# A cached-attention decode layer on one Trainium2 core: the query weights' rows are dealt to the partitions in another way

## The chip, the cores and the metric

One core of a Trainium2 chip runs the kernel. The metric is the device time of one execution in microseconds: the median of 3 runs was 189.68 us before the change (189.66 to 189.79).

## The reference

One token passes through a layer: normalisation, attention over a cache of 16,384 keys and values in 8 key heads with 32 query heads, and then a block of small matrix products. All inputs are bfloat16.

```python
x = A_x                                             # 1 x 1 x 512
q = _layernorm(x) @ wq                              # wq 512 x 4096; 32 heads of 128
scores = einsum("bhqd,bhkd->bhqk", q, k) * 128 ** -0.5   # k, v: 8 heads x 16384 x 128, each for 4 query heads
o = einsum("bhqk,bhkd->bhqd", softmax(scores), v)
h = x + o.reshape(1, 1, 4096) @ wo                  # wo 4096 x 512
n = _layernorm(h)
x1 = n                                              # plus, with one token, a shifted product that is zero
h2 = _gelu(_layernorm(x1) @ w3) @ w4                # w3 512 x 1792, w4 1792 x 512
out = h + x1 + h2
```

The block B shifts its token by one and two places along a sequence of length one. Nothing but padding is left of it, so the kernel does not read `B_w1` and `B_w2`.

## The kernel before

The kernel is written as one straight list of operations for each engine. A small recorder (`Program`) notes what each operation reads and writes, and puts a semaphore wait ahead of an operation that needs it; TensorE's own list (PE below) is run as a loop. No scheduler moves anything: the order on each engine is the order of the code.

All 17 large loads are issued by SyncE (SP), in this order: the query weights in two pieces, keys of pair 0, values of pair 0, keys of pair 1, values of pair 1 and so on, to pair 3 (whose keys come in two halves), then `wo`, `w3` and `w4`. A "pair" is two key heads; its keys, and its values, are 128 partitions x 64 KB, 8 MB in one load. The input `x` (`x4`, 1 KB as 4 rows of 256 B) is loaded by ScalarE's queue (ACT). A load waits on SP until its destination is free. The buffer `vb` holds first the query weights (`wq_sb` is another name for it) and then the values of each pair, so the values of pair 0 wait for the query product to have read the weights. The keys go into a ring `kb_all`, so the keys of pair 1 wait until VectorE (DVE) has transposed the keys of pair 0.

The start, which the change touches, goes like this. PE copies `x` to all partitions: partitions 32q to 32q+31 hold elements 128q to 128q+127, four quarters in all. `row_sums(0, ...)` takes the sums for the mean and the variance, and transposes `hx` into `hT` in 32 x 32 blocks (L550), so that partition 32q+i holds its four elements 128q + 4i + k, k = 0 to 3. L615 normalises them into `xn`, four columns of 128 elements. L615 also waits for both pieces of the weights: it names `("v", 0)` and `("v", 1)` as read. Then PE makes the query in 32 matmuls (L624): for each of 8 banks, the four columns of `xn` against the four weight rows that lie in the same partition. Partition 32q+i must therefore hold the weight rows that belong to its elements. `variance(0)` and small masks are made on DVE and GpSimd (POOL) in between.

The keys of a pair are transposed on DVE (L647) in pieces of 1024 or 2048 words, multiplied with the query on PE (L666), followed by softmax (L676 to L692), the product with the values (L703) and a gathering of the heads. At the end come the products with `wo` (L795), `w3` (L815) and `w4` (L838, L852). Matmuls at L527 and L535 are never read; they only keep PE busy.

The loads of the weights before:

```python
wq_in = A_wq.rearrange("(p k) c -> p (k c)", k=NCH)
for n, (lo, hi) in enumerate(((0, 2048), (2048, NCH * HQ * DH))):
    load("wq", wq_sb[:, lo:hi], wq_in[:, lo:hi], ("v", 1 - n))
load_keys(0)
```

Partition p holds rows 4p to 4p+3, 32 KB that lie together in memory. The first load takes the first 4 KB of each partition (half of its first row), the second the other 28 KB.

Of the kernel before, what the change touches and what calls it, by code (L numbers as in the profile page):

```python
# [365 lines left out]
HQ = 32  # L366
HKV = 8
SK = 16384
DH = 128
REP = HQ // HKV  # L370
FM = 1792
NCH = D // 128
# [18 lines left out]
def bass_sequential_preLN__gqa_block_cached__mixer_s_mlp__decode_kernel(  # L391
# [13 lines left out]
    with ExitStack() as ctx:  # L405
# [50 lines left out]
        hT = sb("hT", [128, NCH, 32], FP32)  # L456
# [18 lines left out]
        wq_sb, wo_sb = vb, kb[0]  # L475
# [11 lines left out]
        def load(name, dst, src, key, by="SP", also=()):  # L487
            P.op(by, lambda e: e.dma_start(dst, src), w=[key, *also], dma=name)  # L488
# [4 lines left out]
        def load_keys(j, y=None):  # L493
            n = 128 * DH
            if y is None:
                load("k", kb_all[:, BASE[j]:BASE[j] + 2 * n], pair_rows(A_k_cache, j), ("r", 0, 0),
                     also=[("r", y, i) for y in range(2) for i in range(RPARTS) if y or i] + [("tail", j)])
            else:
                load(f"k{y}", kb[y][:, :], pair_rows(A_k_cache, j)[:, y * n:(y + 1) * n], ("r", y, 0),
                     also=[("r", y, i) for i in range(1, RPARTS)])  # L500
# [6 lines left out]
        def dve(fn, r=(), w=(), bank=()):  # L507
            return P.op("DVE", fn, r, w, bank)
# [7 lines left out]
        def pe(fn, r=(), w=(), bank=(), also=()):  # L516

            return P.op("PE", fn, r, w, bank, also=also)

        def piece(cuts, m):  # L520
            return [lo <= m < hi for lo, hi in cuts].index(True)
# [16 lines left out]
        def row_sums(i, row, key):  # L538

            h, hk = (hr, "hr") if i else (hx, "hx")  # L540
            if i:
                dve(lambda e: e.scalar_tensor_tensor(h[:, :], row[:, 0:128], 1.0, hx[:, :], ALU.mult, ALU.add,
                                                     accum_out=rs[i][:, 0:1]),
                    r=[key, "hx"], w=[hk, ("rs", i, 0)], bank=[key])
            else:
                dve(lambda e: e.tensor_scalar(h[:, :], row[:, 0:128], 0.0, 0.0, ALU.add, ALU.add,
                                              accum_out=rs[i][:, 0:1]), r=[key], w=[hk, ("rs", i, 0)], bank=[key])
            dve(lambda e: e.scalar_tensor_tensor(xs[:, :], h[:, :], 1.0, h[:, :], ALU.mult, ALU.mult,
                                                 accum_out=rs[i][:, 1:2]), r=[hk], w=["xs", ("rs", i, 1)])
            dve(lambda e: e.transpose(hT[:, :, :].rearrange("p k u -> p (k u)"),  # L550
                                      h[:, :].rearrange("p (i k) -> p k i", k=NCH)), r=[hk], w=["hT"])
            pe(lambda e: e.matmul(n_ps[:, 0:2], mean4[:, :], rs[i][:, :], start=True, stop=True),
               r=[("rs", i, 0), ("rs", i, 1), "mean4"], w=["n"], bank=["mn"])
            dve(lambda e: e.tensor_copy(st[i][:, 0:2], n_ps[:, 0:2]), r=["n"], w=[(("st", i), 0)], bank=["mn"])
# [15 lines left out]


        load("x4", x4[:, :], A_x[0, 0:1, :].rearrange("o (q j) -> (o q) j", q=4), "x4", "ACT")
        wq_in = A_wq.rearrange("(p k) c -> p (k c)", k=NCH)
        for n, (lo, hi) in enumerate(((0, 2048), (2048, NCH * HQ * DH))):
            load("wq", wq_sb[:, lo:hi], wq_in[:, lo:hi], ("v", 1 - n))
        load_keys(0)

        dve(lambda e: e.memset(mean4[:, :], -1.0 / (32 * D)), w=["mean4"])
# [9 lines left out]
            r=["ident", "x4"], w=["quarter"])  # L588
        pe(lambda e: e.matmul(O_ps[0][:, 0:128], quarter[:, :, :].rearrange("p q u -> p (q u)"), x4[:, :],
                              start=True, stop=True), r=["quarter"], w=[("O", 0)], bank=[("O", 0)])  # L590
        row_sums(0, O_ps[0], ("O", 0))
        variance(0)
        act(lambda e: e.activation(scr[0:1, 0:1], mean4[0:1, 0:1], ACTF.Exp), r=["mean4"], w=["scr"])
# [5 lines left out]
             r=["ident_f"], w=["swapped"])  # L599

        dve(lambda e: e.tensor_reduce(row32[:, :], ident_f[:, :].rearrange("p (c r) -> p r c", c=4), AX.X, ALU.add),
            r=["ident_f"], w=["row32"])
        dve(lambda e: e.tensor_reduce(maskdd[:, :], ident_f[:, :].rearrange("p (n d) -> p d n", d=4), AX.X, ALU.add),
            r=["ident_f"], w=["maskdd"])
# [6 lines left out]
        for z, m, key, mk in ((zo, rowgh, "zo", "rowgh"), (zd, maskgh, "zd", "maskgh")):  # L611
# [5 lines left out]
            r=["hT", (("st", 0), 0), (("st", 0), 6)] + [("v", 0), ("v", 1)], w=["xn"])  # L617
# [3 lines left out]
        for i, key in enumerate(keys):  # L621
            P.part("query", i)
            for k in range(NCH):
                pe(lambda e, k=k: e.matmul(row[:, bass.ds(P.b, 512)], copies(xn[:, k:k + 1], 128),  # L624
                                           wq_k[:, k, bass.ds(P.c, REP * DH)], start=(k == 0), stop=(k == NCH - 1)),
                   r=["xn"], also=[("v", 0), ("v", 1)], w=["n" if key == "mn" else key], bank=[key])
        P.part()
        for g in range(2):
            half = banks[64 * g:64 * g + 64, PAIRS * g:PAIRS * g + PAIRS, :].rearrange("p j c -> p (j c)")
            for b in range(2):  # L630
# [3 lines left out]
                    r=["n" if x == "mn" else x for x in keys[PAIRS * g:PAIRS * g + PAIRS]], w=["qcol"],  # L634
                    bank=keys[PAIRS * g:PAIRS * g + PAIRS])
        for a in range(4):
            lo, hi = 32 * a, 32 * a + 32
# [146 lines left out]
        for n, (lo, hi) in enumerate(W4):  # L784
# [4 lines left out]
            r=[("o_m", j) for j in range(PAIRS)], w=["o_f"])  # L789
# [3 lines left out]
        for r_ in range(32):  # L793
            q = r_ % 4
            pe(lambda e, r_=r_, q=q: e.matmul(O_ps[0][32 * q:32 * q + 32, :], copies(o_b[:, r_:r_ + 1], 32),  # L795
                                              wo_sb[:, r_ * D:(r_ + 1) * D], start=(r_ < 4), stop=(r_ >= 28)),
               r=["o_b", ("r", 0, piece(WO, r_))], w=[("O", 0)], bank=[("O", 0)])
        h_ps, hkey = banks[:, 6, :], "spare0"
        dve(lambda e: e.tensor_copy(osum[:, :], O_ps[0][:, :]), r=[("O", 0)], w=["osum"] + [("osum", c) for c in range(4)], bank=[("O", 0)])
        for q in range(4):  # L800
            pe(lambda e, q=q: e.matmul(h_ps[32 * q:32 * q + 32, 0:128], copies(row32[:, 0:1], 32),
                                       osum[:, q * 128:(q + 1) * 128], start=True, stop=True),
               r=["osum", "row32"], w=[hkey], bank=[hkey])
        s = st[1]
        S = ("st", 1)
        unread(2)
        row_sums(1, h_ps, hkey)
        unread_f(512)
        act(lambda e: e.activation(hc[:, :, :], hT[:, :, :], ACTF.Identity, bias=s[:, 0:1], scale=1.0),
            r=["hT", (S, 0)], w=["hc"])  # L810


        for k in range(NCH):
            for q in range(4):
                pe(lambda e, k=k, q=q: e.matmul(s_ps[32 * q:32 * q + 32, 0, 0:FQ], hc[:, k, :],  # L815
                                                w3_sb[:, k, q * FQ:(q + 1) * FQ], start=(k == 0), stop=(k == NCH - 1)),
                   r=["hc", ("r", 1, piece(W3, k))], w=[("s", 0)], bank=[("s", 0)])
# [3 lines left out]
            r=["hr", "xs", (S, 6)], w=["xsum"])  # L821
        unread_f(384)
        for n in range(2):
            lo, hi = n * NHC // 2, (n + 1) * NHC // 2
# [10 lines left out]
           r=["swapped", "xsum"], w=["n"], bank=["mn"])  # L835
        for m in range(NEAR):
            q = m % 4
            pe(lambda e, m=m, q=q: e.matmul(O_ps[1][32 * q:32 * q + 32, :], hcol[:, m, :], w4_sb[:, m, :],  # L838
                                            start=(m < 4), stop=(m >= NEAR - 4)),
               r=[("hcol", 2 * m // NHC), ("r", 1, len(W3) + piece(W4, m))], w=[("O", 1)], bank=[("O", 1)])  # L840
        dve(lambda e: e.tensor_copy(osum[:, :], O_ps[1][:, :]), r=[("O", 1)], w=["osum"], bank=[("O", 1)])
        act(lambda e: e.activation(hg[:, 0:256], hcol[:, 0:8, :].rearrange("p m u -> p (m u)"), ACTF.Identity),
            r=[("hcol", 1)], w=["late", ("hg", 0), ("hg", 1)])
# [6 lines left out]
        for m in range(NEAR, NHC):  # L850
            for o in range(4):
# [4 lines left out]
                   r=["late", ("r", 1, len(W3) + piece(W4, m))], w=["n"], bank=["mn"])  # L856
        act(lambda e: e.activation(fin[:, 0:128], n_ps[0:64, 0:128], ACTF.Identity),
            r=["n"], w=[("fin", 0)], bank=["mn"])
        dve(lambda e: e.tensor_copy(fin[:, 128:256], n_ps[64:128, 0:128]), r=["n"], w=[("fin", 1)])
        P.op("SP", lambda e: e.dma_start(out[0, 0:1, :].rearrange("o (q j) -> (o q) j", q=2), fin[31:33, :]),  # L860
             r=[("fin", 1), ("fin", 0)], w=["out"], dma="out")
# [32 lines left out]
```

## Time and profile before

| | |
|---|---|
| time, median of 3 | 189.68 us (189.66 to 189.79) |
| time of the profiled execution | 189.68 us |
| its span, first to last instruction | 188.2 us |
| granted TensorE clock, mean | 0.90 |
| PE, DVE, ACT, POOL busy | 127.9, 107.9, 14.2, 9.4 us |
| bytes loaded | 79.17 MB, 421 GB/s over the span |
| SP's DMA queue, share of 16 engines' span | 97.9% |

The page divides the span into 40 slices with the busy share of each engine and of the 16 DMA engines. Behind an issue of a DMA it gives the time to landing, and the chain of waits follows the work back from the last instruction. Each large load consists of one piece per partition and of one small completion packet from each DMA engine that took part; the page counts both as packets.

### The profile page before, as it was taken

The numbers are of one execution on the slowest core, as the hardware profiler recorded it, in microseconds if no ns is written. First come the engines' busy times: TensorE is split into PE (matmuls) and PEld (weight loads), VectorE is DVE, ScalarE is ACT, GpSimd is POOL, SyncE is SP. The second block draws the span as 40 slices with busy tenths as digits, with TensorE's granted clock in tenths as the row PEclk, the third lists the DMA queues.
The fourth block names the chain that finished last, engine by engine and source line by source line (L and its number), as shares of the span: only waits on it lengthen the run. The fifth ranks groups of instructions, "written<-read, shape, count | busy, mean of one in ns | idle before, by whom it ended". The sixth has DMA issues, their size and how long they took to land.

```text
span 188.2 us, 2422 instructions
## 1 busy us (share of the span) xinstructions
PE 127.9 (68%) x776; PEld 53.2 (28%) x780; DVE 107.9 (57%) x138; ACT 14.2 (8%) x32; POOL 9.4 (5%) x21
## 2 busy tenths in 40 slices
PE   1019800699965703999775019997986999797984
PEld 1003300243422201344332003442432334343332
DVE  4300651999645009998450069994659894453254
ACT  3000000000020200000012000000220000320012
POOL 1700000000000020000002100000003000000010
PEclk9999995599997885599999855999998899999999
DMA  6999999999999999888999999997999998799994
GB/s 240 457 418 446 446 446 446 446 446 446 446 446 446 446 446 446 362 376 376 446 446 446 446 446 446 446 446 334 446 446 446 557 446 348 334 471 421 404 410 179
DMA packets 2461, 79.19 MB, mean 421 GB/s; under 512 B 282, under 2 KB 284, under 8 KB 924
## 3 DMA queue, kind: packets, MB, share of 16 engines
q1 hardware_dynamic: 2452, 79.17, 97.9%
q8 instruction: 1, 0.02, 0.0%
q10 hardware_dynamic: 8, 0.00, 0.0%
HBM read 79.17 MB, written 0.00 MB: 421 GB/s over the span
## 4 chain that ended last, share of the span: by engine, by line
DMA 44%; PE 31%; DVE 14%; issue 8%; POOL 1%; SPq 0%; ACT 0%; POOLq 0%; DVEq 0%; ACTq 0%
DMA kb<-in_A_k_cache_dram 30%; PE banks L666 18%; DMA vb<-in_A_v_cache_dram 15%; DVE kt L647 8%; PE banks L527 4%; PE banks L703 4%; DVE pt L692 1%; DVE mx L676 1%; PE banks L795 1%; PE banks L660 1%; DVE od L733 1%; PE banks L680 1%; PE banks L535 1%; PE banks L815 1%; SPq L488 0%
## 5 line engine op out<-in xcount | busy, mean ns | idle before, releaser
L647 DVE STREAM_TRANSPOSE kt<-kb 128x1024 int32<-128x1024 int32 (+1 forms) x49 | 71.8, 1534 | 31.9 <-DMA kb<-in_A_k_cache_dram 31.9
L666 PE MATMUL banks<-kt,qn 128*128 x256 | 67.9, 417 | 0.0
L666 PEld LDWEIGHTS banks<-kt,qn 128*128 x256 | 26.4, 103 | 40.0 <-issue 21.1
L527 PE MATMUL banks<-xn 128*128 128x512 bf16 x90 | 22.0, 381 | 0.6 <-issue 0.6
L660 PE MATMUL banks<-qn 128*128 128x512 bf16 x8 | 3.7, 464 | 26.5 <-DVE kt L647 26.2
L703 PE MATMUL banks<-vb,pt 128*32 128x512 bf16 x256 | 16.3, 411 | 0.0
L624 PE MATMUL banks<-vb,xn 128*128 x32 | 9.2, 459 | 9.6 <-DVE xn L615 9.6
L688 ACT ACTIVATE p_sb<-banks,bias 128x1024 bf16<-128x1024 f32 x4 | 4.5, 1114 | 126.0 <-DVE nmh L684 126.0
L692 DVE STREAM_TRANSPOSE pt<-p_sb 64x1024 bf16<-64x1024 bf16 x8 | 9.9, 1239 | 5.4 <-ACT p_sb L688 5.3
L527 PEld LDWEIGHTS banks<-xn 128*128 128x128 bf16 x94 | 8.8, 99 | 12.1 <-issue 4.5
L676 DVE TENSOR_REDUCE mx<-banks 128x1 f32<-128x1024 f32 x4 | 4.9, 1225 | 9.0 <-PE banks L666 9.0
L703 PEld LDWEIGHTS banks<-vb,pt 128*32 128x32 bf16 x256 | 8.0, 103 | 6.3 <-issue 2.0
L631 DVE STREAM_TRANSPOSE kt<-banks 64x1024 f32<-64x1024 f32 x4 | 4.8, 1227 | 7.2 <-PE banks L624 7.2
L660 PEld LDWEIGHTS banks<-qn 128*128 128x128 bf16 x8 | 0.8, 100 | 28.3 <-issue 28.0
L722 POOL TENSOR_TENSOR osum<-osum 128x256 f32<-128x256 f32 x3 | 2.2, 723 | 127.5 <-ACT osum L719 127.5
L624 PEld LDWEIGHTS banks<-vb,xn 128*128 128x128 bf16 x32 | 3.7, 115 | 14.7 <-issue 12.3
L738 PE MATMUL banks<-od,zo 128*32 128x128 f32 x8 | 1.6, 285 | 7.3 <-POOL od L724 6.1
L680 PE MATMUL banks<-mxd,mean 128*128 128x128 f32 x8 | 2.0, 326 | 5.3 <-DVE mxd L677 5.3
L719 ACT ACTIVATE osum<-banks,rowc 128x128 f32<-128x128 f32 x12 | 3.4, 368 | 20.7 <-PE banks L703 20.7
L615 DVE TENSOR_SCALAR xn<-hT,st 128x4 bf16<-128x4 f32 x1 | 0.3, 290 | 6.5 <-DMA vb<-in_A_wq_dram 6.5
L711 PE MATMUL banks<-acc,zd 128*32 128x1 f32 x8 | 0.9, 180 | 4.1 <-DVE pt L692 4.0
L568 POOL TENSOR_TENSOR st<-st,expo 128x1 f32<-128x1 f32 (+1 forms) x2 | 1.3, 636 | 41.3 <-DVE st L566 41.3
(88 smaller groups left out, 46.3 us busy)
## 6 DMA issues: line engine op xcount, KB each, us to landing
kb<-in_A_k_cache_dram SPq DMA_DIRECT2D x2, 4096.0 KB, 20.4
vb<-in_A_wq_dram SPq DMA_DIRECT2D x1, 3584.0 KB, 11.7
kb<-in_A_wo_dram SPq DMA_DIRECT2D x1, 3584.0 KB, 28.5
kb<-in_B_w_dram SPq DMA_DIRECT2D x1, 1792.0 KB, 24.2
kb<-in_B_w_dram SPq DMA_DIRECT2D x1, 896.0 KB, 26.0
kb<-in_B_w_dram SPq DMA_DIRECT2D x1, 640.0 KB, 27.1
vb<-in_A_wq_dram SPq DMA_DIRECT2D x1, 512.0 KB, 3.6
kb<-in_A_wo_dram SPq DMA_DIRECT2D x1, 512.0 KB, 29.4
```

The source lines that it names most:

```text
L527: P.unread = lambda e: e.matmul(banks[:, 7, :], copies(xn[:, 0:1], 128), copies(xn[:, 0:1], 512), start=True, stop=True)
L624: pe(lambda e, k=k: e.matmul(row[:, bass.ds(P.b, 512)], copies(xn[:, k:k + 1], 128), wq_k[:, k, bass.ds(P.c, REP * DH)], start=(k == 0), s ...
L631: dve(lambda e, g=g, b=b, half=half: e.transpose(qcol[64 * g:64 * g + 64, 2 * b:2 * b + 2, :, :].rearrange("p e m u -> p (e m u)"), half.r ...
L647: P.op("DVE", lambda e, t=t, n=n, at=at: e.transpose(kt[:, t * KP:(t + n) * KP].bitcast(I32), kb_all[:, at:at + n * KP].bitcast(I32)), r=[ ...
L660: pe(lambda e: e.matmul(row[:, bass.ds(P.y, 512)], copies(none, 128), copies(none, 512), start=True, stop=False, skip_group_check=True), r ...
L666: pe(lambda e, n=n: e.matmul(row[:, bass.ds(P.y, 512)], qn[:, n, bass.ds(P.q, 128)], key_piece(P.k, n), start=False, stop=(n == 3), skip_g ...
L676: dve(lambda e: e.tensor_reduce(mx[:, :], s_all, AX.X, ALU.max), r=[("s", 0), ("s", 1)], w=["mx"], **both)
L680: pe(lambda e: e.matmul(m_ps[:, 0:128], mean4[:, :], mxd[:, :], start=True, stop=True), r=["mxd", "mean4"], w=["m"], bank=["mn"])
L688: act(lambda e: e.activation(p_sb[:, :], s_all, ACTF.Exp, bias=bias[:, 0:1], scale=float(SCALE), accum_out=acc[:, :]), r=[("s", 0), ("s", ...
L692: dve(lambda e, g=g: e.transpose(pt[64 * g:64 * g + 64, :, :, g, :], p_sb[64 * g:64 * g + 64, :]), r=["p"], w=["pt"])
L703: pe(lambda e, l=l, ct=ct, ch=ch: e.matmul(O_ps[0][32 * ct:32 * ct + 32, :], pt[:, l, ch, :, :].rearrange("p g u -> p (g u)"), tiles[:, l ...
L719: act(lambda e, c=c: e.activation(osum[:, c * 128:(c + 1) * 128], O[:, c * 128:(c + 1) * 128], ACTF.Identity, scale=rowc[:, c:c + 1]), r=[ ...
```

## The change

The weight rows are dealt out otherwise. Partition 32q+i now holds row 128q+i as its first row, and rows 128q+32+3i to 128q+34+3i as the other three. The first load takes the first row of every partition, whole (8 KB), and the second load the other three (24 KB, which lie together in memory). On the memory side, a load is now described by three dimensions: 4 quarters, 1 MB apart; 32 partitions of each, 8 KB apart in the first load and 24 KB in the second; and the bytes of one partition. Before, it was two: 128 partitions, 32 KB apart, and the bytes. On the side of the partitions there are 128 of them, as before.

The elements of `x` have to follow, so the transposition of `hx` for the first normalisation is cut in two: block 0 (elements 128q+i), and blocks 1 to 3 (elements 128q+32+3i+k). The second call of `row_sums`, at the end of the kernel, stays as it was.

```diff
-            dve(lambda e: e.transpose(hT[:, :, :].rearrange("p k u -> p (k u)"),
-                                      h[:, :].rearrange("p (i k) -> p k i", k=NCH)), r=[hk], w=["hT"])
+            for lo, hi in ((0, NCH),) if i else ((0, 1), (1, NCH)):
+                dve(lambda e, lo=lo, hi=hi: e.transpose(
+                    hT[:, lo:hi, :].rearrange("p k u -> p (k u)"),
+                    h[:, 32 * lo:32 * hi].rearrange("p (i k) -> p k i", k=hi - lo)), r=[hk], w=["hT"])
...
-        wq_in = A_wq.rearrange("(p k) c -> p (k c)", k=NCH)
-        for n, (lo, hi) in enumerate(((0, 2048), (2048, NCH * HQ * DH))):
-            load("wq", wq_sb[:, lo:hi], wq_in[:, lo:hi], ("v", 1 - n))
+        wq_in = A_wq.rearrange("(q d) c -> q d c", q=4)
+        for n, (lo, hi) in enumerate(((0, 1), (1, NCH))):
+            load("wq", wq_sb[:, lo * HQ * DH:hi * HQ * DH],
+                 wq_in[:, 32 * lo:32 * hi, :].rearrange("q (i k) c -> q i (k c)", k=hi - lo), ("v", 1 - n))
         load_keys(0)
```

On SP, at the start of the program, the first loads stand like this (- before, + after; `vb` is the buffer of the weights and values, `kb` that of the keys; the numbers are the destination's shape in elements of 2 bytes):

```order
-L488 DMA vb<-in_A_wq_dram 128x2048
-L488 DMA vb<-in_A_wq_dram 128x14336
+L488 DMA vb<-in_A_wq_dram 128x1x4096
+L488 DMA vb<-in_A_wq_dram 128x1x12288
 L488 DMA kb<-in_A_k_cache_dram 128x32768
 L488 DMA vb<-in_A_v_cache_dram 128x32768
```

Nothing moves in SP's list: still two weight loads, then the keys and the values. Their sizes change from 4 KB and 28 KB of each partition to 8 KB and 24 KB.

On DVE, near the start, `row_sums(0, ...)` and what follows it stood like this before:

```order
L546 TENSOR_SCALAR hx,rs<-banks 128x128
L548 SCALAR_TENSOR_TENSOR xs,rs<-hx 128x128
L550 STREAM_TRANSPOSE hT<-hx 128x128
L554 COPY st<-banks 128x2
L560 SCALAR_TENSOR_TENSOR st<-st 128x1
```

And like this after:

```order
L546 TENSOR_SCALAR hx,rs<-banks 128x128
L548 SCALAR_TENSOR_TENSOR xs,rs<-hx 128x128
L551 STREAM_TRANSPOSE hT<-hx 128x32
L551 STREAM_TRANSPOSE hT<-hx 128x96
L556 COPY st<-banks 128x2
L562 SCALAR_TENSOR_TENSOR st<-st 128x1
```

One transposition has become two, of a quarter and three quarters of the columns. All other rows of every engine stand as before, with line numbers 2 or 3 higher.

## The prediction

> **What bounds the kernel now.** I read the page's DMA part first, because 79 MB in 189.68 us is a lot for one core. The columns are packets, MB, and share of 16 engines' span.
>
> ```profile
> span 188.2 us, 2422 instructions
> DMA packets 2461, 79.19 MB, mean 421 GB/s; under 512 B 282, under 2 KB 284, under 8 KB 924
> q1 hardware_dynamic: 2452, 79.17, 97.9%
> q10 hardware_dynamic: 8, 0.00, 0.0%
> ```
>
> SP's queue (q1) keeps all 16 DMA engines busy for 97.9% of the span. Stretches cut out by the view of windows show whether that is one rate or a mixture (the last two numbers are the share of the DMA engines and GB/s):
>
> ```profile
> 12.95:32.30 19.35, 9.19 (x32) 3.67 (x32) 6.06 (x10) 0.00 (x0) 0.00 (x0) 0.89 1.00 434
> 32.30:70.90 38.60, 26.16 (x146) 10.39 (x147) 22.70 (x21) 2.71 (x7) 1.57 (x3) 0.85 1.00 435
> 101.20:129.00 27.80, 17.64 (x67) 6.91 (x67) 17.90 (x12) 1.50 (x5) 1.57 (x3) 0.82 1.01 434
> 129.00:148.00 19.00, 15.20 (x110) 6.29 (x110) 13.75 (x14) 2.71 (x7) 1.57 (x3) 0.91 1.09 469
> 176.00:186.00 10.00, 7.91 (x101) 3.31 (x102) 4.63 (x16) 1.67 (x4) 0.71 (x1) 1.00 0.96 401
> ```
>
> In the long stretches it is one rate: 434 GB/s at a share of 1.00, 27.1 GB/s for each engine. (The 469 beside a share of 1.09 and the 401 have the edges of large packets in them.) PE and DVE have room in each stretch, so this kernel is a queue of bytes. It stays one only if each load is issued before the one ahead of it has drained. SP's timeline has the issues (start, us, what), and the chain of waits has what they became:
>
> ```profile
> 0.74 0.87 SPq L488 DMA_DIRECT2D vb<-in_A_wq_dram  x2
> 1.66 0.42 SPq L488 DMA_DIRECT2D kb<-in_A_k_cache_dram  x1
> 22.93 0.33 SPq L488 DMA_DIRECT2D vb<-in_A_v_cache_dram  x1
> 45.77 0.33 SPq L488 DMA_DIRECT2D kb<-in_A_k_cache_dram  x1
> 64.26 0.33 SPq L488 DMA_DIRECT2D vb<-in_A_v_cache_dram  x1
> 84.47 0.33 SPq L488 DMA_DIRECT2D kb<-in_A_k_cache_dram  x1
> 101.26 0.33 SPq L488 DMA_DIRECT2D vb<-in_A_v_cache_dram  x1
> 118.67 9.29 SPq L488 DMA_DIRECT2D kb<-in_A_k_cache_dram  x2
> 139.97 0.33 SPq L488 DMA_DIRECT2D vb<-in_A_v_cache_dram  x1
> 147.74 0.80 SPq L488 DMA_DIRECT2D kb<-in_A_wo_dram  x2
> 157.64 1.78 SPq L488 DMA_DIRECT2D kb<-in_B_w_dram  x4
> ```
> ```profile
> 1.66 30.55 DMA kb<-in_A_k_cache_dram
> 45.77 25.13 DMA kb<-in_A_k_cache_dram
> 101.26 27.72 DMA vb<-in_A_v_cache_dram
> ```
>
> An 8 MB load takes 19.35 us at the full rate (the first window holds exactly the keys of pair 0). The second keys took 25.13 us from issue, the third values 27.72, so they stood 5.8 and 8.4 us in the queue. The values of pair 0 were issued at 22.93, 9.3 us before the first keys had landed (1.66 + 30.55 = 32.21). The chain ends in the last weights:
>
> ```profile
> 186.29 0.12 PEld L852 LDWEIGHTS banks<-kb,kt 128*32 128x32 bf16 x8 [0.19 <-DMA kb<-in_B_w_dram]
> ```
>
> PE waits 0.19 us for the last piece of `w4`, 2 us before the end. What lengthens any one engine's queue lengthens the kernel, since a load has landed only when all its engines have.
>
> **How the change alters the loads.** The weights are 512 + 3584 KB in both kernels. The rows of the DMA issues give KB and time to landing:
>
> ```profile
> vb<-in_A_wq_dram SPq DMA_DIRECT2D x1, 3584.0 KB, 11.7
> vb<-in_A_wq_dram SPq DMA_DIRECT2D x1, 512.0 KB, 3.6
> x<-in_A_x_dram ACTq DMA_DIRECT2D x1, 1.0 KB
> out_dram<-kt SPq DMA_DIRECT2D x1, 1.0 KB
> ```
>
> The question is over how many engines a load is spread, and the packet counts answer it for what is in this kernel. SP's timeline has 17 large loads; 128 pieces each are 2,176 packets, and the store of the output has two rows, so two more. The 2452 of q1 leave 274: 16 completions for each of 17 loads (272), and 2 for the store. The load of `x` has 4 rows and 8 packets on q10: 4 pieces, 4 completions. The 282 packets under 512 B are the same sum (274 + 8). So an engine completes where it took part: a transfer with 128 rows outermost ran on 16 engines, one with 4 on four, one with 2 on two.
>
> After the change the destination still has 128 partitions outermost, but the source has 4 (the quarters, 1 MB apart, which do not join with the 32 rows inside). No transfer of this trace has sides that differ. The bounds are 16 engines, as for 128 rows, at no cost, and four, as for `x`. I take four: both sides must be cut into the same shares, and the outermost step of the source can be cut into four only. [...]
>
> **The sum.** On four engines, each carries 4096 / 4 = 1024 KB of weights instead of 4096 / 16 = 256 KB. The extra 768 KB (786,432 B) at 27.1 GB/s are **29.0 us**. I take both loads to fall on the same four, so that their shares add up; no row tells which engines took part in one. On different ones the fullest would carry 768 KB of weights, 512 KB more than now, and the sum would be 19.3 us (209.0 us).
>
> Could the rest absorb this? Twelve engines skip the weights, have their part of keys 0 about 19.35 us after they start, and stand idle, since SP cannot go further: the values of pair 0 need `vb`, which the query matmuls must have read. Their start waits for the weights:
>
> ```profile
> 12.95 0.29 DVE L615 TENSOR_SCALAR xn<-hT,st 128x4 bf16<-128x4 f32 x1 [6.50 <-DMA vb<-in_A_wq_dram]
> 13.63 9.19 PE L624 MATMUL banks<-vb,xn 128*128 x32 [9.60 <-DVE xn L615]
> 3.30 0.40 DVE L550 STREAM_TRANSPOSE hT<-hx 128x128 f32<-128x128 f32 x1
> ```
>
> L615 moves from 12.95 to about 41.9, the issue of the values (9.98 us behind it) to 51.9. The four engines get to keys 0 at 41.9 and need 19.35 us more: keys 0 land at 61.2 instead of 32.2, and the values stand in the queue 9.3 us before that, as now. From there DVE's transposes, the next issue and all others hang on landings that the four engines set. They see today's queue, 29.0 us later, with the same slack; the other twelve run ahead and wait. Nothing of the 29.0 us is given back, up to the last `w4`.
>
> The other edits cost nothing. One 0.40 us transposition becomes two: the same columns in all, so at least 0.40 us, and at most 0.80 if each cost as much as the whole. DVE idles 6.50 us ahead of L615, longer afterwards; without four engines the 6.50 us still cover it. Behind the pair on DVE stand the copy of the sums and the variance, which have the same cover. There are as many pieces (256), of 8 and 24 KB instead of 4 and 28 KB. PE's 32 matmuls read the same shapes.
>
> The profiled execution took 189.68 us, which is also the median; 1.5 us of it lie outside the 188.2 us span and stay. 189.68 + 29.0 = **218.7 us** (span 217.2).
>
> The rate of the four engines is the uncertain term, since they work alone. From above, the 469 GB/s row (29.3 each) brings the 1,048,576 B in 35.8 us; less the 9.7 us of now, that is +26.1, or 215.8 us. From below, the 401 row (25.1 each) gives 41.8 us, +32.1, or 221.8 us. I take 434, which three rows show, and keep 215.5 to 222.
>
> **The rivals.**
> *All 16 engines anyway.* The spread follows the partitions' side, and the change does nothing to the queue: equal bytes, equal pieces, 189.7 us. For it: all 17 loads with 128 partitions got 16 completions. Against it: in all of those the source had 128 outermost too. Chance 6%.
> *Faster: 16 engines, and a quicker start.* The first load was issued at 0.74 and landed 3.6 us later, of which its 512 KB need 1.2 us at the full rate; the second landed 8.55 us behind it (1.19 + 11.7 against 4.34), and its 3584 KB need 8.46. So what is lost lies in the first load alone: 2.4 us. If a fifth of that is due to its 4 KB pieces, and 8 KB pieces save it, every landing comes 0.5 us earlier: 189.2 us. It decides from 0.4 us on. Most of the 2.4 us must be the way to the first byte, and four engines would bury the gain. Chance 3%.
> *Half the loss.* Eight engines share the weights, or four run at twice the rate when alone: 512 KB per engine at the old rate, 256 KB more than now, 9.7 us, 199.4 us. Against it: the rate is the same 434 in stretches with very different work on the other engines, which looks like each DMA engine's own. Chance 4%.
> *Two engines.* 2048 KB each, 67.7 us more, about 257 us. Only the output's two rows ran on two. Chance 1%. The two loads on different fours (209.0 us) get 1% as well.
>
> **How the numbers follow.** The same four engines: 85%, of which I count 4 points outside 215.5 to 222; the range then holds 81%. About 0.2% (0.4 us) is what a measurement of this kernel can tell from no change. Faster 3% (the quicker start), the same 6% (16 engines), slower 91% (the rest).
>
> **What would show it.** With four engines, q1 has 2 x 12 = 24 completions fewer: 2428 packets, and 258 under 512 B. The weights land at about 41.9 us. The DMA share falls to a quarter between about 22 us, when twelve engines are through with keys 0, and 52 us, and is 79.17 / (16 x 27.1 GB/s x 217.2 us) = 84% over the span. L615 still waits for the weights, now for some 35 us, and the times from there on, row by row, are those of now plus 29. Wrong would be 2452 packets again with a span near 188; or 2428 with weights that land before 38 or after 45 us, which would show another rate of four engines alone; or a later landing that comes less than 26 us later than now, which would show that the queue gave something back.

## The result, and the profile after

The changed kernel takes 260.73 us, the median of 6 runs (258.03 to 263.92), against 189.67 us before (189.42 to 189.84). Without the two slowest of the six (263.00 and 263.92 us), which show a second, slower state, the ratio is 1.368 (95% interval 1.364 to 1.372). The forecast was 218.7 us, 215.5 to 222.0: the right direction, and much too little. The profiled execution took 258.03 us, so 68.35 us more than the 189.68 us of the profiled one before.

The page of the changed kernel, with the 40 slices of the DMA engines' busy share and the GB/s that they moved:

```profile
span 256.5 us, 2427 instructions
DMA  7899989222222299989899899899998999998992
GB/s 161 172 162 199 256 165 183 57 57 69 73 65 107 92 368 409 409 317 388 388 450 460 368 480 450 378 480 429 399 480 368 440 419 460 450 470 354 409 416 92
DMA packets 2437, 79.19 MB, mean 309 GB/s; under 512 B 258, under 2 KB 260, under 8 KB 772
q1 hardware_dynamic: 2428, 79.17, 82.4%
```

The packet counts are those forecast for four engines: 2428 on q1, 24 completions fewer, and 258 under 512 B. The slices show what was not forecast. In the first seven, nearly all DMA engines are busy, and yet only 161 to 256 GB/s move. In the next seven, a quarter of them is busy, as expected, but at 57 to 107 GB/s instead of four times 27.1. Windows inside the two stretches, and one far behind them (the last two numbers are DMA share and GB/s):

```profile
25.00:45.00 20.00, 0.00 (x0) 0.00 (x0) 0.00 (x0) 0.00 (x0) 0.00 (x0) 1.00 1.00 203
50.00:80.00 30.00, 0.00 (x0) 0.00 (x0) 0.00 (x0) 0.00 (x0) 0.00 (x0) 1.00 0.25 67
140.00:220.00 80.00, 61.93 (x344) 25.17 (x345) 57.17 (x50) 5.40 (x14) 3.14 (x6) 0.87 1.00 433
```

Sixteen busy engines at 203 GB/s, four at 67 (16.8 each), and later all at the old 433. VectorE's timeline has the two landings of the start:

```profile
81.16 0.29 DVE L618 TENSOR_SCALAR xn<-hT,st 128x4 bf16<-128x4 f32 x1 [72.96 <-DMA vb<-in_A_wq_dram]
100.38 12.27 DVE L650 STREAM_TRANSPOSE kt<-kb 128x2048 int32<-128x2048 int32 x7 [5.83 <-DMA kb<-in_A_k_cache_dram]
```

The weights land at 81.2 us, where 41.9 was forecast. From there on SP's timeline is the old one, moved:

```profile
91.11 0.33 SPq L488 DMA_DIRECT2D vb<-in_A_v_cache_dram  x1
113.85 0.33 SPq L488 DMA_DIRECT2D kb<-in_A_k_cache_dram  x1
226.00 1.76 SPq L488 DMA_DIRECT2D kb<-in_B_w_dram  x4
```

These three issues stood at 22.93, 45.77 and 157.64: 68.2, 68.1 and 68.4 us later. All of the loss is in the loads of the weights, and none of it is given back. The question is why four engines that were to bring 108 GB/s brought 67, and less than that beside the keys: there the median piece of 24 KB took 2.01 us, 12.2 GB/s for each engine.

### The profile page after: what moved, and what is told of

Read it like the earlier page. It is cut to its first block, busy times and chain, and to the rows that moved or that the text cites. A ratio compares the mean times of both kernels' runs of the same rounds, so it can differ in the third digit from the quotient of the medians.

```text
span 256.5 us, 2427 instructions
## 1 busy us (share of the span) xinstructions
PE 128.6 (50%) x780; PEld 53.0 (21%) x780; DVE 109.7 (43%) x139; ACT 14.2 (6%) x32; POOL 9.3 (4%) x21
## 3 DMA queue, kind: packets, MB, share of 16 engines
q1 hardware_dynamic: 2428, 79.17, 82.4%
## 4 chain that ended last, share of the span: by engine, by line
another core or an unknown queue 31%; PE 27%; DMA 21%; DVE 13%; issue 7%; POOL 0%; ACT 0%; POOLq 0%; DVEq 0%; SPq 0%; ACTq 0%
PE banks L669 13%; DMA vb<-in_A_v_cache_dram 11%; DMA kb<-in_A_k_cache_dram 10%; DVE kt L650 6%; PE banks L627 4%; PE banks L527 3%; PE banks L706 3%; DVE pt L695 1%; DVE mx L679 1%; DVE zo L615 1%; PE banks L798 1%; PE banks L663 1%; DMA x<-in_A_x_dram 1%; DVE kt L634 0%
## 5 line engine op out<-in xcount | busy, mean ns | idle before, releaser
L618 DVE TENSOR_SCALAR xn<-hT,st 128x4 bf16<-128x4 f32 x1 | 0.3, 289 | 73.0 <-DMA vb<-in_A_wq_dram 73.0
L527 PE MATMUL banks<-xn 128*128 128x512 bf16 x94 | 22.9, 381 | 0.0
L527 PEld LDWEIGHTS banks<-xn 128*128 128x128 bf16 x94 | 8.8, 99 | 12.2 <-issue 4.1
## 6 DMA issues: line engine op xcount, KB each, us to landing
kb<-in_B_w_dram SPq DMA_DIRECT2D x1, 640.0 KB, 27.1
```

What stands on the lines that cost most here:

```text
L527: P.unread = lambda e: e.matmul(banks[:, 7, :], copies(xn[:, 0:1], 128), copies(xn[:, 0:1], 512), start=True, stop=True)
```

## The experiments

Theory 1 was the **source**: the four streams read 1 MB apart and meet in memory. Theory 2 was the **destination**: groups of partitions share an entrance, a way in for the DMA engines' bytes, that lets through what one engine moved in the kernel before, 27.1 GB/s, and partitions p and p + 32 of one half (0 to 63, or 64 to 127) share the same one. No trace shows an entrance; what the runs below show is the rates of loads into different partitions: 212 GB/s into 32 partitions, 222 into 0 to 63, 418 into 32 to 95, beside the 434 of 128 partitions. By theory 2, if each of the four engines has one quarter, they walk through partitions i, 32+i, 64+i and 96+i about in step, so two and two of them would meet all the time, and with engines that write keys as well; a load of 128 partitions would give every engine an entrance of its own. Unless a text says otherwise, a run below was timed once, and is to be set against 189.6 to 190.2 us for the kernel before and 258 to 264 for the changed one. Where the time of a single piece is given, it is that of the piece's packet in the run's trace.

### Each quarter a load of its own

```diff
         for n, (lo, hi) in enumerate(((0, 1), (1, NCH))):
-            load("wq", ...)
+            for q in range(4):
+                load("wq", wq_sb[32 * q:32 * q + 32, lo * HQ * DH:hi * HQ * DH],
+                     wq_in[q, 32 * lo:32 * hi, :].rearrange("(i k) c -> i (k c)", k=hi - lo), ...)
```

> The dealing of the changed kernel, but each quarter of each weight load is a load of its own: 32 partitions on both sides, 8 loads instead of 2. Both theories expect 16 engines (two partitions each). Theory 1, the source: four streams that read 1 MB apart hold each other up in memory. Here all engines read one quarter, pieces that lie together, so the weights come at the full rate, land near 13 us, and the time is 189.7 (189.2 to 190.5). Theory 2, the destination: engines that write into the same group of partitions share one entrance of 27 GB/s. In a load of 32 partitions the 16 engines have 8 such groups, so the weights come at about half rate: 19.3 instead of 9.7 us, and the time is 199 (197 to 201).

Measured over 3 rounds: 199.41 us (199.33 to 199.50), 1.051 times the kernel before (1.049 to 1.053). The queue's row and a window:

```profile
q1 hardware_dynamic: 2548, 79.17, 98.1%
8.00:21.00 13.00, 0.00 (x0) 0.00 (x0) 0.00 (x0) 0.00 (x0) 0.65 (x2) 1.00 1.03 212
```

2548 packets are 8 loads of 32 pieces and 16 completions each, beside the other 2164: 16 engines took part. All were busy, the source lay together, and they moved 212 GB/s, about half of the 434 of before, or 26.5 for each of the 8 entrances that theory 2 counts. Theory 2 had forecast this: half the rate, and 199 us. Theory 1 had forecast the full rate and 189.7 us.

### Another distance at the source

```diff
-        wq_in = A_wq.rearrange("(q d) c -> q d c", q=4)
+        wq_in = A_k_cache[0].rearrange("h s d -> (h s d)")
...                          # quarters 524288 + 12288 elements apart, else the same two loads
```

> The loads of the changed kernel, on four engines, with the same partitions and sizes; only the source differs: bytes of the key cache, with the four quarters 1 MB + 24 KB apart instead of 1 MB (the query is then made of other numbers). Theory 1 (source): the four streams no longer meet, each engine reaches 27.1 GB/s, the weights land near 42 us, 218.7 us as predicted. Theory 2 (destination): nothing changes, the weights land near 81 us, 258 to 264 us.

Measured: 263.02 us; `xn`'s instruction waited until 86.16 us for the bytes in place of the weights. Moving the source did not help; that the bytes came 5 us later than in the profiled execution of the changed kernel is within what that kernel's own six times differ by (5.9 us).

```profile
86.16 0.29 DVE L621 TENSOR_SCALAR xn<-hT,st 128x4 bf16<-128x4 f32 x1 [77.81 <-DMA vb<-in_A_k_cache_dram]
```

### A bad distance at the source, with 16 engines

```diff
-        wq_in = A_wq.rearrange("(p k) c -> p (k c)", k=NCH)
+        wq_in = A_k_cache[0].rearrange("h s d -> (h s d)").rearrange("(p e) -> p e", p=128)
```

> The kernel before, with its two loads of 128 partitions on 16 engines; only the source differs: bytes of the key cache, with the rows of neighbouring partitions 256 KB apart instead of 32 KB, so that engines which work on partitions four apart read 1 MB apart (the query is made of other numbers). Theory 1 (source): the 16 streams meet in memory worse than four did; at the 65 GB/s that the four got, the weights land near 67 us and the time is about 243. Theory 2 (destination): each engine writes its own partitions as before, 189.7 us.

Measured: 190.21 us, with the weights there at 13.63 us instead of 12.95. Here the source costs 0.7 us at most, where theory 1 had forecast 53 us. With the run before, theory 1 falls.

### Four engines, neighbouring partitions

```diff
+            for b in range(8):
+                load("wq", wq_sb[16 * b:16 * b + 16, lo * HQ * DH:hi * HQ * DH],
+                     wq_in[:, 32 * lo + 4 * b * w:32 * lo + 4 * (b + 1) * w, :].rearrange(...), ...)
```

> Four engines with the source quarters 1 MB apart, as in the changed kernel, but in 16 loads of 16 partitions, so that at any time the four engines write four neighbouring groups of four partitions instead of partitions 32 apart (rows are dealt otherwise, so the output is another). Theory 1 (source): as slow as the changed kernel, weights near 81 us, 258 to 264. Theory 2 (destination): the four don't share an entrance with each other, only at times with the engines that load the keys; the weights land between 42 and 55 us, 219 to 232 us.

Measured: 233.29 us, the weights there at 56.33: a little over the upper end of theory 2, and far from theory 1. Windows before the keys start, three times beside them, and after the twelve other engines are through with them:

```profile
5.00:11.00 6.00, 0.00 (x0) 0.00 (x0) 3.37 (x8) 0.00 (x0) 3.36 (x5) 1.00 0.25 107
19.00:24.00 5.00, 0.00 (x0) 0.00 (x0) 0.00 (x0) 0.00 (x0) 0.00 (x0) 1.00 0.94 216
24.40:26.90 2.50, 0.00 (x0) 0.00 (x0) 0.00 (x0) 0.00 (x0) 0.00 (x0) 1.00 0.99 423
33.00:45.00 12.00, 0.00 (x0) 0.00 (x0) 0.00 (x0) 0.00 (x0) 0.00 (x0) 1.00 0.86 182
50.00:55.00 5.00, 0.00 (x0) 0.00 (x0) 0.00 (x0) 0.00 (x0) 0.00 (x0) 1.00 0.27 118
```

Four engines alone move 107 GB/s, the rate of the prediction. (The 2484 packets on q1 have four completions for each of the 16 loads.) Beside the keys the total falls to about 200, with one full recovery: 423 GB/s between 24.4 and 26.9 us. The pieces show where it belongs. Of the second eight loads, the first (partitions 0 to 15) has pieces of 0.91 to 1.09 us, and the third (32 to 47), once its first pieces are through, of 0.91 to 0.93; the pieces of the second (16 to 31) and the fourth (48 to 63) rise to 1.90 and 1.95. Keys that start with the third's free pieces take 2.42 to 2.52 us for 64 KB, as in the kernel before (2.42); those beside the second take up to 4.83. Theory 2 gives such a pattern if the four engines are the same that write the keys of partitions 0 to 15 and 32 to 47, so that nobody else writes there; which engine writes where is not in the trace. So there are two losses, and the next two runs take them apart.

### The keys only after the weights

```diff
+        P.op("SP", lambda e: e.nop(), r=[("v", 0), ("v", 1)])
         load_keys(0)
```

> The changed kernel, with keys 0 issued only when the weights have landed, so that the four engines work alone throughout. In the changed kernel they got 11 to 14 GB/s each beside the keys and 16 to 17 when the keys were through. Shared entrances: they get the 16 to 17 from the start, the weights land at 64 to 68 us instead of 81, the keys some 21 us later, 243 to 248 us. If the keys beside them had cost nothing, the weights would still land at 81, and the time would be about 281.

The changed kernel with this line took 242.36 us, just under the range; the weights were there at 63.03 instead of 81.16, a little before the 64 to 68 expected, so the keys beside them had cost 18.1 us. Making the keys wait even made the changed kernel faster. The same line (it then names all 16 loads), with the 16 loads of 16 partitions:

> The 16 loads of 16 partitions (four engines, which write four neighbouring groups of four partitions; rows dealt otherwise, so the output is another), with keys 0 issued only when the weights have landed: neither the four among themselves nor the keys meet at an entrance. Shared entrances: each engine reaches 27.1 GB/s, the weights land near 42 us as the prediction had it, the keys some 21 us later at 63, 219 to 223 us. If four engines are slow in themselves, the weights land at 64 us or later and the time is 245 or more.

Measured: 222.38 us. The weights and the keys in the run with the changed kernel's loads, then in the one with neighbouring partitions, and a window of the latter:

```profile
63.03 0.29 DVE L619 TENSOR_SCALAR xn<-hT,st 128x4 bf16<-128x4 f32 x1 [54.84 <-DMA vb<-in_A_wq_dram]
84.98 17.90 DVE L651 STREAM_TRANSPOSE kt<-kb 128x2048 int32<-128x2048 int32 x12 [8.31 <-DMA kb<-in_A_k_cache_dram]
```
```profile
42.98 0.29 DVE L622 TENSOR_SCALAR xn<-hT,st 128x4 bf16<-128x4 f32 x1 [36.50 <-DMA vb<-in_A_wq_dram]
64.71 17.90 DVE L654 STREAM_TRANSPOSE kt<-kb 128x2048 int32<-128x2048 int32 x12 [8.84 <-DMA kb<-in_A_k_cache_dram]
```
```profile
15.00:42.00 27.00, 0.00 (x0) 0.00 (x0) 0.00 (x0) 0.00 (x0) 0.00 (x0) 1.00 0.25 107
```

Where by theory 2 neither the four engines nor the keys meet, four engines bring the weights at 42.98, as good as the 41.9 of the prediction. Both runs use four engines and read the same rows at the same distances; what differs is the partitions that the four write at one time, and that there are 16 loads instead of two. The changed kernel's partitions cost another 20.1 us.

### Sixty-four partitions, two choices

The dealing and the piece sizes of before, with the two loads cut by partitions:

```diff
-            load("wq", wq_sb[:, lo:hi], wq_in[:, lo:hi], ("v", 1 - n))
+            for b, (at, to) in enumerate(((0, 64), (64, 128))):      # or ((32, 96), (0, 32), (96, 128))
+                load("wq", wq_sb[at:to, lo:hi], wq_in[at:to, lo:hi], ...)
```

> The kernel before with its dealing and piece sizes, but each weight load cut into two loads of 64 partitions, 0 to 63 and 64 to 127. Shared entrances, with partitions 32 apart at the same one: a load of 64 partitions reaches 8 entrances like one of 32, half rate, 199.4 us (198 to 201). If small loads are slow in themselves (16 engines with fewer pieces each), four loads of 64 lose less than eight of 32, which gave 199.4: 190 to 196 us.

> The kernel before with its dealing and piece sizes, but each weight load cut into three: partitions 32 to 95, then 0 to 31, then 96 to 127. Shared entrances: the middle 64 partitions reach all 16 and go at the full rate, the two outer loads reach 8 each and go at half; 4.8 us more in all, 194.5 us (193 to 196). If small loads are slow in themselves, three loads lose more than two: at least the time of the halves.

Measured: halves 201.22 us, just over the range, and middle 198.97, 3 us over its range. The packets on q1 (2484 and 2516) show 16 engines for each load. The halves, at twice the partitions of a quarter, are no better than the quarters (199.41), which small loads being slow in themselves does not explain. The middle is better than the halves in spite of more loads, but 4.5 us over the expected time. The stretch around its middle load, and then that of the outer ones:

```profile
5.00:9.00 4.00, 0.00 (x0) 0.00 (x0) 1.44 (x7) 0.00 (x0) 3.42 (x5) 1.00 1.17 418
9.00:17.00 8.00, 0.00 (x0) 0.00 (x0) 0.00 (x0) 0.00 (x0) 0.00 (x0) 1.00 0.95 198
```

The same stretch of the halves:

```profile
5.00:9.00 4.00, 0.00 (x0) 0.00 (x0) 1.44 (x7) 0.00 (x0) 3.42 (x5) 1.00 1.04 222
```

Partitions 32 to 95 go at 418 GB/s, 0 to 63 at 222, with as many engines and bytes in a load. The 418 stands beside a share of 1.17, so the edges of pieces are in it, but the pieces say the same: those of 28 KB that start between 5.4 and 8.0 us in the middle load take 1.06 us at the median, as in the kernel before, and those of the halves 2.24. That tells the choice of partitions apart from the size of a load. The 198 of the outer loads is below 217, half of the 434, and the last of their pieces ends at 21.4 us, 4 us after most. The keys are not the reason in that window, since their first piece starts at 16.9 us; why the outer loads are slower than expected stays open.

### Whole rows alone

```diff
-        for n, (lo, hi) in enumerate(((0, 2048), (2048, NCH * HQ * DH))):
+        for n, (lo, hi) in enumerate(((0, 4096), (4096, NCH * HQ * DH))):
```

> The kernel before with its dealing (partition p holds rows 4p to 4p+3), but the weight loads cut as in the changed kernel: one whole row (8 KB) of each partition first, then the other three (24 KB). Both sides have 128 partitions outermost, so 16 engines at their own entrances. If the spread over the engines is all that costs, whole rows alone change nothing: 189.7 us (189.3 to 190.1), q1 with 2452 packets. If the cut itself matters, a difference of more than 0.4 us either way shows it; the quicker start of the prediction's faster rival would give 189.2.

Measured over 5 rounds: 189.72 us, 1.0003 times the kernel before (0.9993 to 1.0013), with 2452 packets on q1. Pieces of 8 and 24 KB are neither better nor worse than 4 and 28. There is nothing in whole rows that a better version of the changed dealing could bring, and no run beat the kernel before.

## Why the prediction was wrong

**The bound** was right. The kernel is a queue of bytes, and the later issues moved by the same 68 us as the first landing.

**The spread over engines** was right: 2428 packets, so each weight load, with 128 partitions on one side and 4 quarters on the other, has four completions instead of 16. That both sides must be cut into the same shares was my argument for it; the runs show it for 4 against 128 here, and for 4 against 16 in the loads of neighbouring partitions, and no more than that.

**The rigid move** was right: twelve engines ran ahead and waited, and SP's issue of the values came 9.95 us behind L618 as it had come 9.98 us behind L615. The two transpositions on DVE took 0.39 us together. The pace of the twelve was not: they were to be through with their keys at about 22 us, and their last piece ended at 48.5. That cost nothing more, since the four engines were later still.

**The rate of the four engines** is the step that failed: "I take 434, which three rows show, and keep 215.5 to 222". That put 27.1 GB/s for each engine, 108 for four, into the sum; the changed kernel's four had 67 alone and less beside the keys, and the term of 29.0 us became 68.2. Both ends came from stretches in which 16 engines load 128 partitions, so they could only show how much an engine moves in such a load. I had called the rate the own property of each DMA engine. It depended as much on the place that was written (16 engines moved 222 GB/s into partitions 0 to 63 and 418 into 32 to 95), and no row of before could tell the two apart, since there every large load writes 128 partitions. The landing of the weights splits the loss:

| weights there at | us | step |
|---|---|---|
| before, 16 engines | 12.95 | |
| four engines, neighbouring partitions, alone | 42.98 | 30.0: the spread (29.0 forecast) |
| four engines, the changed kernel's two loads, alone | 63.03 | 20.1: their partitions (by theory 2 they meet in pairs) |
| the same beside the keys (the changed kernel) | 81.16 | 18.1: the keys beside them |

The sum is 68.2 of 68.35 us. Each row is one execution, and that of the changed kernel is the fastest of six (258.03 to 263.92 us), so the last step can be some us larger; with neighbouring partitions the keys cost 13.4 us (56.33 against 42.98). The two last steps were missing from the prediction. Its rival of two engines, at about 257 us, comes near the measured time by chance: two engines would leave 28 completions fewer, and 24 are missing. For the first of the two missing steps, theory 2 fits the rates: 212 and 222 GB/s where it counts 8 entrances, 418 for the middle 64 partitions, where it counts 16. If each pair had shared 27.1 GB/s evenly all the time, the four would have had 54 GB/s; they had 67. I estimate from this 67, and from the pieces of 24 KB in the run with the four engines alone, that the engines of a pair are out of step and write alone part of the time: the pieces took from 0.91 to 1.94 us, a fifth of them under 1.0 and a third over 1.7, where with neighbouring partitions all 128 took 0.91.

**What stays open** is why the keys suffer so widely. In the run with neighbouring partitions, the load at 19 to 24 us writes 16 partitions, so by theory 2 at most four of the twelve key engines should be in its way. With those eight engines sharing four entrances (108 GB/s) and the other eight free (217), 325 GB/s were to be expected, and 216 were measured. No eight were free: the twelve pieces of keys that started between 19.6 and 20.7 us all took 4.38 to 4.83 us instead of 2.42. Something that theory 2 alone does not explain held up the others too; whether it lies on the reading or the writing side was not tried.

## What to carry to other kernels

Count a load's rate twice: by the engines that take part (16 completions where both sides had 128 outermost, four where the source had 4), and by the partitions that they write at the same time (four engines moved 67 GB/s in the changed kernel's loads, 107 into neighbouring partitions). Here a source written in three dimensions, with 4 outermost, turned two loads of 128 partitions into loads of four engines, and the instruction list, which shows the destination's shape, does not tell it; the completion packets do, 4 a load instead of 16. And when a prediction takes a rate from a trace, ask what every row that showed it had in common.

## What the runs showed of the hardware that I had not expected

- Four DMA engines moved 67 GB/s in the changed kernel's loads of 128 partitions, and 107 in loads of 16 neighbouring partitions.
- Loads of partitions 0 to 63 moved 222 GB/s, those of 32 to 95 moved 418; pieces of 28 KB took 2.24 us in the one and 1.06 in the other.
- Beside the four engines of the weights the whole queue was slow: 16 busy engines moved 203 GB/s for 20 us, where the kernel before moved 434; all 96 pieces of keys that the other twelve brought by 48.5 us took 4.12 us or more, instead of 2.42.
- Reading rows 256 KB apart instead of 32 KB, from another tensor, delayed 4 MB by 0.7 us.
